# A sliding-window attention and MLP block on one core: the last chunk's output finished by VectorE and plain stores, its PSUM places, the bias matmul, the tile adds of chunk 1, and a new written order

## The chip, the cores and the metric

The kernel runs on one core of a Trainium2 chip. The metric is the device time of one execution in microseconds, as the median of several runs; lower is better. The core's engines each work through their own list of instructions in order: PE (TensorE, matmuls), DVE (VectorE), ACT (ScalarE), POOL (GpSimd) and SP (SyncE, which issues DMAs here). They wait for each other by semaphores.

## What is computed

With x of 2048 rows (positions) by 640, the output is x plus an attention branch plus an MLP branch, both on the layer-normed rows xn. The attention has 32 heads of 20; each position looks at itself and 7 earlier positions, 2 apart.

```python
xn = _layernorm(x, axis=-1)
q, k, v = (xn @ wqkv) split into 32 heads of 20
idx = pos[:, None] - 2 * arange(8)[None, :]
logits = einsum("bhsd,bhswd->bhsw", q, k[idx]) * 20 ** -0.5   (masked where idx < 0)
A = einsum("bhsw,bhswd->bhsd", softmax(logits), v[idx]) @ wo
B = gelu(xn @ w1 + b1) @ w2 + b2
return x + A + B
```

All inputs and the output are bfloat16; w1 is 640 by 1536, w2 is 1536 by 640.

## The kernel before, in words

The 2048 rows are worked in four chunks of 512 (n = 0 to 3), each of four blocks of 128 rows. Features lie on the partitions, rows along the free dimension: xnT, qT, kT, vT and the output of attention oT are each five tiles of 128 features by 512 rows. The feature order of q, k, v is permuted so that four partitions hold one head's features in every tile, 20 in five tiles.

For each chunk:

- Statistics (bn_stats on DVE for chunks 0 and 1, ACT sums for 2 and 3), xn, and its transposition: by PE in chunk 0, by DMA transposes issued on SP (L293) in the others.
- q, k, v projections: five matmuls into a PSUM tile from the pool psA (4 places, L102), cast to SBUF by ACT (`do_pj`, `do_pc`, L340 and L404; chunk 0 in smaller pieces, L353 to L399).
- Products of q and the shifted k on DVE (`do_qk`, L437), 8 shifts in two tiles `half[0]` and `half[1]` of 4 shifts by 5 feature tiles by 512 rows; each instruction does half a chunk's rows for 4 shifts.
- The sum over a head's features: some of the five feature tiles are first added on DVE (`do_pa`, L469: tile 1 onto tile 0 and 3 onto 2 in one instruction; `do_pb`, L474), the rest is summed on PE by matmuls with the 0/1 matrix `head_of` (`do_lg`, L483). `LEVEL` says for each chunk how many adds come first: level 0 leaves five tiles to PE (40 matmuls), level 1 three (24), level 2 two (16), level 3 one (8). Level 1 has four `pa` instructions on DVE, level 2 two `pb` more, level 3 four `pb` more. These matmuls have 32 output rows each; the four blocks go to four different sets of 32 rows.
- Softmax: maximum and subtraction on DVE (L524, L530), exponent on ACT (L540), sums on DVE (L544, L546), reciprocal by Ln and Exp on ACT (L552, L553), product on DVE (L558). The weights `attn` are then spread over the partitions by four DMAs per chunk on SP (`do_xd`, `do_xs`, L577), in chunks 1 and 3 into rows of x_sb that are no longer needed.
- Products with the shifted v on DVE (`do_av`, L592, eight per chunk, into the same two `half` tiles) and their sums (`do_add`, L601, three, and `do_ot`, L606), which give oT.
- The MLP: 12 hidden tiles, five matmuls each (`do_f1`, L613), gelu on ACT (`do_ge`, L629).
- Output of chunks 0 to 2: transposed, T = w2 times hidden plus wo times oT in five pieces (`do_t`, L708), with the bias added by ACT (`do_u`, L711), turned by a DMA transpose on SP (`do_ut`, L715), and added onto the output in memory by an accumulating DMA on POOL (`do_ud`, L720). The output rows have been set to x by a plain DMA earlier (`do_xp`, L302).
- Output of chunk 3: rows on the partitions, per block 17 matmuls of 512 columns ("lo", L656) and 17 of 128 columns ("hi", L661). Blocks 0 and 1 are cast by ACT (`do_oc`, L668, L669) and added onto the output by accumulating DMAs on POOL (`do_od`, L673); their rows have been set to x by `do_xp` of chunk 3 and had b2 added by another accumulating DMA (`do_xb`, L306). Blocks 2 and 3 are added to x + b2 by DVE (`direct`, L680; x + b2 is made in place by `do_xl`, L310) and stored by plain DMAs on SP (L729, L733) and ACT (L744). The "lo" of block 0 and the "hi" of blocks 0 and 1 share the two-bank PSUM tile that the logits use (psL); the "hi" of blocks 2 and 3 share one place of psA, in which the first matmul alone opens the bank (`opened`).

The order of the instructions on PE, DVE, ACT and SP is written out by hand: the string `ORDER` is a list of pieces, and each piece emits its instructions in that order, so that each engine's list is the pieces that use it, in turn. `pj123`, for instance, is projection 2 (v), tile 3 of chunk 1; `lg2` the logit matmuls of chunk 2; `av110` a v product of chunk 1; `ot1` its oT; `f12_5` the hidden tile 5 of chunk 2; `t104` the last piece of T (with oT) for output tile 0 of chunk 1; `o324` the last piece (with oT) of block 2 of chunk 3; `ohi` all "hi" matmuls of block 3. POOL's instructions are placed by the framework. PSUM has eight banks: psA 4, psL 2, psO 2.

Of the kernel before, what the change touches and what calls it, by code (L numbers as in the profile page):

```python
# [11 lines left out]
ALU = mybir.AluOpType  # L12
AX = mybir.AxisListType
BF16 = mybir.dt.bfloat16
# [15 lines left out]
LASTB = S // P - 1  # L30
DIRECT = 2
WARM = 10
RB = 32
# [3 lines left out]
LEVEL = (1, 0, 2, 3)  # L37
# [6 lines left out]
tp01a gb3 tp01b tc01a tc01b gb4 gd gc0 ge tb hj100 st02a st02 rs02 st03a gc1 st03 rs03 xn02 tp02 gc4 ho b1 xn03 st11a  # L44
st13a st10a st12a st10 hc100 st11 hj102 tp03 st13 tc02 tc03 st12 hj101 hc101 hj110 hc110 hc102 hj010 pk rs1 rc1 hj012
hc012 xn12 tc12 hj112 hc112 hj011 hj111 hc010 qk000 xn10 tc10 hc111 hj210 hc210 hc011 hj200 qk001 hc200 xn11 tc11
hj212 hc212 qk010 pad11 hj202 f10_5 hj201 f10_10 xn13 hc202 hc201 f10_4 f10_0 ge0_5 f10_7 ge0_0 tc13 pj102 pa010 ge0_7
pc102 pa001 qk011 pj111 pc111 pj112 pj113 pc112 pa000 pa011 lg0 mask m0a mx0a ge0_4 pc113 ge0_10 ex0a pj103 pc103
pj104 pc104 ldx m0b mx0b ex0b ss0a ri0a pj110 pc110 ss0b ri0b pj114 pc114 pj100 pc100 ld2 pj101 at0a at0b xd0 pc101
qk110 qk100 su22 hj211 hc211 f10_1 pj121 su23 ge0_1 qk101 f10_6 qk111 ge0_6 f10_8 su21 ge0_8 su20 pc121 xs0 f10_9  # L50
f10_2 f11_7 ge0_9 ge0_2 ng2 ge1_7 f10_3 f11_9 pj124 lg1 av030 av000 ldo t040 av001 sq23 sq22 ge0_3 sq21 pc124 sq20 rs2
rc2 av031 av010 m1 f11_2 xp1 av011 av021 av020 mx1 ad00 t000 t041 xn22 tc22 pj123 pc123 xn23 tc23 f11_0 ge1_0 ge1_2
t042 xn21 tc21 f10_11 ge0_11 xn20 tc20 t001 t002 f11_5 ge1_5 pad12 ge1_9 f11_10 ge1_10 t003 ex1 ss1 pj122 f11_11 pj120
pc120 t043 pc122 pj210 pc210 ri1 at1 pj214 pc214 ad01 xp0 xd1 pj220 pc220 pj211 pc211 xp2 su30 ad02 ot0 pj201 pc201
pj204 pc204 su31 xs1 pj212 pc212 pj224 pj213 pc224 pj202 su32 su33 ng3 av111 pc213 pj203 sq32 t044 u04 av110 av121 xp3
av130 av100 t004 u00 ut00 sq31 pj200 pc200 t010 av101 t011 av120 t012 t013 t020 sq30 av131 t014 u01 ut01 sq33 f11_1
rs3 rc3 t021 t022 t023 t024 t030 t031 t032 t033 xn31 t034 tc31 ad10 pad21 xn33 tc33 ad11 pc203 ad12 ot1 ud00 f11_4
ud01 pc202 qk201 ge1_1 ge1_11 xn30 qk211 qk200 f11_8 f12_11 f12_9 qk210 pa211 tc30 pa200 pa210 xn32 tc32 pad22 ge1_8
ge2_9 pa201 f12_3 ge2_11 f11_6 ge1_6 ge1_4 f12_7 pad31 pb212 u02 pj320 pc320 ge2_7 pj304 pc304 pj311 pc311 pb202 pj313
pc313 pj312 pc312 pj222 u03 pc222 xl pj302 pc302 pj301 pj310 pj300 pc310 ge2_3 f13_2 pc300 pc301 pj314 pc314 pj322  # L60
pj303 pc303 pj321 lg2 f11_3 ge3_2 ge1_3 qk310 m2 ut02 f13_8 ge3_8 xb3 f12_5 pa301 t100 pc322 f13_6 t120 pj221 t101
t102 ge2_5 mx2 t121 f12_8 qk300 ex2 ss2 ri2 pa300 t103 pc221 ut03 ut04 ud02 at2 xd2 qk311 xs2 t104 ge2_8 f13_9 ge3_9
t122 t123 u10 f13_10 ge3_10 f13_7 ge3_7 qk301 ud03 pa311 pa310 f13_1 t110 ge3_1 ge3_6 t111 t112 t113 pj323 f12_1 pb302
pj223 pb312 pb304 pc223 pc321 ud04 pb314 t114 u11 pc323 ut10 ut11 f13_0 lg3 ud10 av200 t124 u12 t140 t141 m3 mx3 t130
t131 av210 ut12 t142 ex3 ss3 t143 pj324 av230 ri3 at3 t132 t133 t134 t144 ge3_0 av211 u13 av201 av220 f12_0 ge2_0
ge2_1 pc324 f13_4 ut13 f13_3 f12_4 av221 av231 ad20 ad21 u14 xd3 f13_5 ge2_4 ge3_3 ut14 o310 f12_6 ad22 ot2 ge3_5
ge3_4 o311 o312 ud11 ud12 ud13 ud14 f12_2 xs3 ge2_6 ge2_2 f12_10 pad32 ge2_10 o320 t210 t211 t212 t200 t201 t202
f13_11 ge3_11 t203 t204 t213 t214 u20 ut20 ud20 u21 ut21 ud21 av311 av301 t220 t221 t222 t230 av310 av321 o321 t223
t224 u22 ut22 ud22 t231 t232 t233 t234 u23 ut23 ud23 o330 o331 t240 t241 t242 o300 o301 o313 av330 av320 av300 av331
ad31 t243 t244 u24 ut24 ud24 ad30 o322 o323 ad32 ot3 o302 o303 o314 o304 o324 o332 dc dd o333 o334 ohi oclo ochi oc31  # L70
od31 oc30 ochd od30
# [4 lines left out]
def kernel(  # L76
# [37 lines left out]
    outp = ctx.enter_context(tc.tile_pool(name="outp", bufs=2))  # L114
# [7 lines left out]
    b_rt = consts.tile([RB, P], BF16, name="b_rt")  # L122
# [173 lines left out]
    def rows(n):  # L296
        cs = slice(n * BPC, min((n + 1) * BPC, LASTB + 1 - DIRECT))
        return cs, out_sd.rearrange("(b p) d -> p b d", p=P)[:, cs, :]
# [5 lines left out]
    def do_xb(n):  # L304
        cs, dst = rows(n)
        nc.gpsimd.dma_start(dst, b2bc[:].unsqueeze(1).to_broadcast([P, cs.stop - cs.start, D]), accum_op=ALU.add)  # L306

    def do_xl():
        rows_ = x_sb[:, LASTB + 1 - DIRECT :, :]
        nc.vector.tensor_tensor(  # L310
            out=rows_, in0=rows_, in1=b2bc[:].unsqueeze(1).to_broadcast([P, DIRECT, D]), op=ALU.add
        )
# [149 lines left out]
    def do_b1():  # L462
        nc.vector.tensor_copy(bT[:], tiles["tb"][:, 0 : FT + KT])
# [420 lines left out]
```

## Time and profile before

The median of 3 runs is 209.16 us (208.89 to 209.57). The profile shows one execution in detail.

| what | value |
|---|---|
| time of the profiled execution | 209.39 us |
| its span, first to last instruction | 207.2 us |
| granted TensorE clock | 1.000 |
| ACT_TABLE_LOAD on ACT (L174) | x12, 15.4 us |
| DVE q products (L437) | x16, 44.4 us |
| DVE v products (L592) | x32, 45.6 us |
| DVE sums to oT (L601) | x12, 33.6 us |
| DVE tile adds (L469) | x12, 14.1 us |
| accumulating stores on POOL (L720) | x15, 19.3 us |

The page gives each engine's busy time and its share of the span, then the busy share of 40 slices in tenths, then a chain of waits traced back from the last instruction. Matmuls are pipelined: each is shown with its depth (379 ns for 512 columns), while the next starts earlier, so for the pace one takes the starts of neighbours. In a timeline row the columns are start, length, engine, line, operation, out<-in, shapes and count, and in brackets the idle time before the row with what ended it.

### The profile page before, as it was taken

The numbers are of one execution on the slowest core, as the hardware profiler recorded it, in microseconds if no ns is written. First come the engines' busy times: TensorE is split into PE (matmuls) and PEld (weight loads), VectorE is DVE, ScalarE is ACT, GpSimd is POOL, SyncE is SP. The second block draws the span as 40 slices with busy tenths as digits, with TensorE's granted clock in tenths as the row PEclk, the third lists the DMA queues.
The fourth block names the chain that finished last, engine by engine and source line by source line (L and its number), as shares of the span: only waits on it lengthen the run. The fifth ranks groups of instructions, "written<-read, shape, count | busy, mean of one in ns | idle before, by whom it ended". The sixth has DMA issues, their size and how long they took to land.

```text
span 207.2 us, 2936 instructions
## 1 busy us (share of the span) xinstructions
PE 201.7 (97%) x1137; PEld 106.8 (52%) x1156; DVE 182.6 (88%) x155; ACT 126.4 (61%) x232; POOL 23.9 (12%) x36
## 2 busy tenths in 40 slices
PE   8999999999999999999999999999999999999993
PEld 3999654644444555444455544444444444444552
DVE  2889994799799899999999989999899999999611
ACT  5778967999879877658685537571658621220120
POOL 2000000000000000420002400002040220224050
PEclk9999999999999999999999999999999999999999
DMA  6995879186063358479324800073472970285455
GB/s 211 389 395 180 60 209 394 39 187 209 0 186 67 130 118 211 103 99 86 69 27 52 75 3 0 0 156 73 53 69 45 157 110 3 51 76 51 54 37 115
DMA packets 36607, 23.56 MB, mean 114 GB/s; under 512 B 24946, under 2 KB 34418, under 8 KB 36594
## 3 DMA queue, kind: packets, MB, share of 16 engines
q1 hardware_dynamic: 26464, 18.91, 36.2%
q0 software_dynamic: 8480, 2.62, 16.5%
q10 hardware_dynamic: 1650, 1.84, 2.5%
q8 instruction: 9, 0.15, 0.3%
q14 instruction: 4, 0.03, 0.1%
HBM read 10.00 MB, written 5.24 MB: 74 GB/s over the span
## 4 chain that ended last, share of the span: by engine, by line
PE 68%; DVE 14%; ACT 8%; DMA 6%; issue 1%; SPq 0%; DVEq 0%; ACTq 0%
PE T L708 18%; PE hps L613 15%; PE pps L340 15%; DVE half L592 10%; PE gps L384 6%; PE lo L656 5%; DMA x_sb<-attn 3%; DMA xnT<-xn 3%; PE idle L450 2%; ACT hT L629 2%; PE tail L656 2%; PE L L483 1%; ACT trash L222 1%; PE gps L353 1%; DVE half L601 1%
## 5 line engine op out<-in xcount | busy, mean ns | idle before, releaser
L613 PE MATMUL hps<-xnT,w_sb 128*128 128x512 bf16 x236 | 55.5, 379 | 0.4 <-ACT hT L629 0.2
L437 DVE TENSOR_TENSOR half<-qT,kT 128x5120 bf16<-128x5120 bf16 x16 | 44.4, 2820 | 2.0 <-PE L L483 1.0
L708 PE MATMUL T<-hT,w_sb 128*128 128x512 bf16 x173 | 41.9, 379 | 0.4 <-issue 0.2
L613 PEld LDWEIGHTS <-w_sb 128*128 128x128 bf16 x240 | 23.3, 98 | 27.9 <-issue 0.9
L720 POOL DMA_DIRECT2D out_dram<-x_sb x15 | 19.3, 1286 | 92.2 <-DMA x_sb<-x_sb 91.5
L629 ACT ACTIVATE hT<-hps,bT 128x512 bf16<-128x512 f32 x36 | 23.8, 689 | 9.0 <-PE hps L613 9.0
L708 PEld LDWEIGHTS <-w_sb 128*128 128x128 bf16 x180 | 17.4, 98 | 21.0 <-issue 0.4
L592 DVE TENSOR_TENSOR half<-vT,ax 128x2560 bf16<-128x2560 bf16 x16 | 23.0, 1484 | 2.5 <-ACT vT L404 2.5
L711 ACT ACTIVATE x_sb<-T,bT 128x512 bf16<-128x512 f32 x15 | 10.3, 690 | 20.9 <-PE T L708 20.9
L592 DVE TENSOR_TENSOR half<-vT,x_sb 128x2560 bf16<-128x2560 bf16 x16 | 22.6, 1485 | 0.2 <-DMA x_sb<-attn 0.2
L601 DVE TENSOR_TENSOR half<-half,half 128x5120 bf16<-128x5120 bf16 x8 | 22.3, 2820 | 0.1
L340 PE MATMUL pps<-xnT,wv_sb 128*128 128x512 bf16 x73 | 18.4, 379 | 0.1
L708 PE MATMUL T<-oT,wo 128*128 128x512 bf16 x75 | 18.3, 379 | 0.0
L340 PE MATMUL pps<-xnT,wq_sb 128*128 128x512 bf16 x74 | 17.8, 379 | 0.1
L340 PE MATMUL pps<-xnT,wk_sb 128*128 128x512 bf16 x72 | 17.5, 379 | 0.2
L174 ACT ACT_TABLE_LOAD x12 | 15.4, 1283 | 0.9 <-PEq L868 0.7
L469 DVE TENSOR_TENSOR half<-half 128x2048 bf16<-128x2048 bf16 x12 | 14.1, 1218 | 0.0
L264 ACT ACTIVATE xn<-x_sb,nmr,rstd 128x640 bf16<-128x640 bf16 x12 | 11.0, 921 | 4.1 <-DVE nmr L254 2.8
L340 PEld LDWEIGHTS <-wv_sb 128*128 128x128 bf16 x75 | 8.8, 117 | 7.6
L340 PEld LDWEIGHTS <-wq_sb 128*128 128x128 bf16 x75 | 8.7, 118 | 7.6 <-issue 0.6
L340 PEld LDWEIGHTS <-wk_sb 128*128 128x128 bf16 x75 | 8.8, 117 | 7.4
L404 ACT CAST kT<-pps 128x512 bf16<-128x512 f32 x15 | 8.7, 581 | 6.1 <-PE pps L340 6.1
(104 smaller groups left out, 239.1 us busy)
## 6 DMA issues: line engine op xcount, KB each, us to landing
w_sb<-in_B_w_dram SPq DMA_DIRECT2D x4, 960.0 KB, 10.2
ax<-attn SPq DMA_DIRECT2D x8, 256.0 KB, 4.8
x_sb<-attn SPq DMA_DIRECT2D x8, 256.0 KB, 4.6
out_dram<-x_sb POOLq DMA_DIRECT2D x15, 128.0 KB, 3.8
x_sb<-in_A_x_dram SPq DMA_DIRECT2D x1, 1280.0 KB, 7.6
out_dram<-x_sb ACTq DMA_DIRECT2D x2, 640.0 KB, 5.3
wq_sb<-in_A_wqkv_dram SPq DMA_DIRECT2D x1, 800.0 KB, 4.8
wk_sb<-in_A_wqkv_dram SPq DMA_DIRECT2D x1, 800.0 KB, 6.9
```

Of the source, the lines that this page charges most:

```text
L174: nc.scalar.preload_act_table_set(name)
L340: nc.tensor.matmul(ps[:], lhsT=wqkv_p[which][:, ti, to, :], rhs=xnT[:, ti, :], start=(ti == 0), stop=(ti == KT - 1),)
L384: nc.tensor.matmul(ps[:, to - a, :], lhsT=wqkv_p[which][:, ti, to, :], rhs=tiles["xnT", 0][:, ti, pair * 2 * P : (pair + 1) * 2 * P], star ...
L437: nc.vector.tensor_tensor(out=half[h][:, :, :, cs], in0=q[:, :, at].unsqueeze(1).to_broadcast([P, W // 2, KT, 2 * P]), in1=window(k, h, at ...
L469: nc.vector.tensor_tensor(out=even, in0=even, in1=odd, op=ALU.add)
L592: nc.vector.tensor_tensor(out=half[h][:, :, :, cs], in0=window(qkv_tile(n, 2), h, cs), in1=ax_view(n)[:, j, ws, :].unsqueeze(2).to_broadca ...
L601: nc.vector.tensor_tensor(out=a, in0=a, in1=b, op=ALU.add)
L613: nc.tensor.matmul(ps[:], lhsT=w1_sb[:, ti, ft * P : (ft + 1) * P], rhs=tiles["xnT", n][:, ti, :], start=(ti == 0), stop=(ti == KT - 1),)
L629: nc.scalar.activation(hT, tiles["hps", n, ft][:], ACT.Gelu_apprx_tanh, bias=bT[:, ft : ft + 1], scale=1.0)
L656: nc.tensor.matmul(out_ps(bl, False), lhsT=lhs, rhs=rhs[:, 0:CH], start=pc == 0 and k == 0, stop=final)
L708: nc.tensor.matmul(ps[:], lhsT=lhs, rhs=rhs, start=pc == 0 and k == 0, stop=pc == 4 and k == len(srcs) - 1)
L720: nc.gpsimd.dma_start(dst, src, accum_op=ALU.add)
```

## The change

- `LEVEL` of chunk 1 goes from 0 to 1: four `pa` pieces (L469) are new, `lg1` has 24 matmuls for 40.
- All four blocks of chunk 3 are finished as blocks 2 and 3 were: DVE adds PSUM and x + b2 (`do_dc`) and a plain DMA stores the block (`do_dd`); `do_oc`, `do_od` and their tiles go. `half[1]` has room for four blocks instead of two. `do_xl` now makes x + b2 for the four blocks in two pieces; `do_xb` and the `do_xp` of chunk 3 go.
- Every "lo" and "hi" has a PSUM place of its own: block 0 the two banks of psL, blocks 1 and 2 the four places of psA, block 3 the two of psO.
- The bias rows are turned by a plain matmul with the identity instead of a transpose, from a tile of 128 rows whose unused rows are zero.
- `ORDER` is a new list throughout; it is cut to its last lines here.

```diff
--- before.py
+++ after.py
@@ -27,48 +27,45 @@
 EPS = 1e-5
 MASKED = -1e9
 MW = 16
-LASTB = S // P - 1
-DIRECT = 2
 WARM = 10
-RB = 32
 TURNED = 4
 PARTS = (2, 1, 1, 1)
 
-LEVEL = (1, 0, 2, 3)
+LEVEL = (1, 1, 2, 3)
 ACT_STATS = (2, 3)
 
 COLS = ((0, 2), (2, 4), (4, 5))
 
 ORDER = """
...
-t224 u22 ut22 ud22 t231 t232 t233 t234 u23 ut23 ud23 o330 o331 t240 t241 t242 o300 o301 o313 av330 av320 av300 av331
-ad31 t243 t244 u24 ut24 ud24 ad30 o322 o323 ad32 ot3 o302 o303 o314 o304 o324 o332 dc dd o333 o334 ohi oclo ochi oc31
-od31 oc30 ochd od30
...
+u20 ut20 ud20 t234 u23 t210 t211 t212 t213 t214 t220 t221 t222 t223 t224 u21 ut21 o312 o313 o321 u22 ut22 o330 o322
+ud21 o331 t240 t241 t242 o323 t243 t244 o332 o333 ot3 o303 o304 ud22 o324 dl0 o314 u24 ut23 ut24 ud23 ud24 dl2 o334
+dh0 dd0 dh2 dd2 ohi dl1 dh1 dd1 dl3 dh3 dlo dhi
 """.split()
 
 
@@ -111,7 +108,6 @@
     axp = ctx.enter_context(tc.tile_pool(name="axp", bufs=1))
     otp = ctx.enter_context(tc.tile_pool(name="otp", bufs=1))
     hp = ctx.enter_context(tc.tile_pool(name="hp", bufs=18))
-    outp = ctx.enter_context(tc.tile_pool(name="outp", bufs=2))
 
 
     x_sb = wts.tile([P, NCH * BPC, D], BF16, name="x_sb")
@@ -119,7 +115,7 @@
     w1_sb = wts.tile([P, KT, F], BF16, name="w1_sb")
     w2_sb = wts.tile([P, FT, D], BF16, name="w2_sb")
     wo2 = wts.tile([P, KT, D], BF16, name="wo2")
-    b_rt = consts.tile([RB, P], BF16, name="b_rt")
+    b_rt = consts.tile([P, P], BF16, name="b_rt")
     nc.gpsimd.memset(b_rt[:], 0.0)
     b2bc = consts.tile([P, D], BF16, name="b2bc")
     wqkv_v = A_wqkv.rearrange("(t p) n -> p t n", p=P)
@@ -294,21 +290,17 @@
 
 
     def rows(n):
-        cs = slice(n * BPC, min((n + 1) * BPC, LASTB + 1 - DIRECT))
+        cs = slice(n * BPC, (n + 1) * BPC)
         return cs, out_sd.rearrange("(b p) d -> p b d", p=P)[:, cs, :]
 
     def do_xp(n):
         cs, dst = rows(n)
         (nc.scalar if n else nc.sync).dma_start(dst, x_sb[:, cs, :])
 
-    def do_xb(n):
-        cs, dst = rows(n)
-        nc.gpsimd.dma_start(dst, b2bc[:].unsqueeze(1).to_broadcast([P, cs.stop - cs.start, D]), accum_op=ALU.add)
-
-    def do_xl():
-        rows_ = x_sb[:, LASTB + 1 - DIRECT :, :]
+    def do_xl(pair):
+        rows_ = x_sb[:, (NCH - 1) * BPC + 2 * pair : (NCH - 1) * BPC + 2 * pair + 2, :]
         nc.vector.tensor_tensor(
-            out=rows_, in0=rows_, in1=b2bc[:].unsqueeze(1).to_broadcast([P, DIRECT, D]), op=ALU.add
+            out=rows_, in0=rows_, in1=b2bc[:].unsqueeze(1).to_broadcast([P, 2, D]), op=ALU.add
         )
 
 
@@ -456,11 +448,11 @@
             )
 
     def do_tb():
-        tiles["tb"] = psL.tile([P, 2 * W * P], BF16, tag="L", name="tb")
-        nc.tensor.transpose(tiles["tb"][:, 0:RB], b_rt[:], ident[0:RB, 0:RB])
+        tiles["tb"] = psL.tile([P, W, P], F32, tag="L", name="tb")
+        nc.tensor.matmul(tiles["tb"][:, 0, 0 : FT + KT], lhsT=b_rt[:], rhs=ident[:, 0 : FT + KT], start=True, stop=True)
 
     def do_b1():
-        nc.vector.tensor_copy(bT[:], tiles["tb"][:, 0 : FT + KT])
+        nc.vector.tensor_copy(bT[:], tiles["tb"][:, 0, 0 : FT + KT])
 
     def do_pa(n, h, c):
 
@@ -633,16 +625,12 @@
 
 
     def out_ps(bl, hi):
-        first = lambda: psL.tile([P, W, P], F32, tag="L", name="tail")
-        if bl == 0 or (hi and bl == 1):
-            ps = get("tail", first)[:].rearrange("p w c -> p (w c)")
-            return ps[:, CH + bl * P : CH + (bl + 1) * P] if hi else ps[:, 0:CH]
-        key = "hi" if hi else ("lo", bl)
-        pool, tag = (psO, "o") if key == ("lo", BPC - 1) else (psA, "acc")
-        ps = get(key, lambda: pool.tile([P, CH], F32, tag=tag, name="hi" if hi else "lo"))
-        return ps[:, (bl - BPC + DIRECT) * P : (bl - BPC + DIRECT + 1) * P] if hi else ps[:]
-
-    opened = set()
+        if bl == 0:
+            both = get("first", lambda: psL.tile([P, W, P], F32, tag="L", name="both"))[:].rearrange("p w c -> p (w c)")
+            return both[:, CH:D] if hi else both[:, 0:CH]
+        pool, tag = (psO, "o") if bl == BPC - 1 else (psA, "acc")
+        ps = get(("out", bl, hi), lambda: pool.tile([P, CH], F32, tag=tag, name="hi" if hi else "lo"))
+        return ps[:, 0 : D - CH] if hi else ps[:]
 
     def do_o(bl, pc, parts):
         n, cs = NCH - 1, slice(bl * P, (bl + 1) * P)
@@ -651,34 +639,25 @@
         else:
             srcs = [(tiles["oT", n][:, t, cs], wo2[:, t, :]) for t in range(KT)]
         for k, (lhs, rhs) in enumerate(srcs):
-            final = pc == 4 and k == len(srcs) - 1
-            if "lo" in parts:
-                nc.tensor.matmul(out_ps(bl, False), lhsT=lhs, rhs=rhs[:, 0:CH], start=pc == 0 and k == 0, stop=final)
-            if "hi" in parts:
-                bank = bl // 2
-                first = bank not in opened
-                opened.add(bank)
+            for hi in parts:
                 nc.tensor.matmul(
-                    out_ps(bl, True), lhsT=lhs, rhs=rhs[:, CH:D], start=first, stop=final, skip_group_check=True
+                    out_ps(bl, hi),
+                    lhsT=lhs,
+                    rhs=rhs[:, CH:D] if hi else rhs[:, 0:CH],
+                    start=pc == 0 and k == 0,
+                    stop=pc == 4 and k == len(srcs) - 1,
                 )
 
-    def do_oc(bl):
-        osb = outp.tile([P, D], BF16, tag="osb", name="osb")
-        tiles["osb", bl] = osb
-        nc.scalar.copy(osb[:, 0:CH], out_ps(bl, False))
-        nc.scalar.copy(osb[:, CH:D], out_ps(bl, True))
-
-    def do_od(bl):
+    def do_dc(bl, hi):
+
+        b, cs = (NCH - 1) * BPC + bl, slice(CH, D) if hi else slice(0, CH)
+        room = half[1][:].rearrange("p w t c -> p (w t c)")[:, bl * D : (bl + 1) * D]
+        nc.vector.tensor_tensor(out=room[:, cs], in0=out_ps(bl, hi), in1=x_sb[:, b, cs], op=ALU.add)
+
+    def do_dd(bl, cs, eng):
         b = (NCH - 1) * BPC + bl
-        nc.gpsimd.dma_start(out_sd[b * P : (b + 1) * P, :], tiles["osb", bl][:], accum_op=ALU.add)
-
-    def direct(bl, hi):
-
-        b = (NCH - 1) * BPC + bl
-        room = half[1][:].rearrange("p w t c -> p (w t c)")[:, (bl % 2) * D : (bl % 2 + 1) * D]
-        cs = slice(CH, D) if hi else slice(0, CH)
-        nc.vector.tensor_tensor(out=room[:, cs], in0=out_ps(bl, hi), in1=x_sb[:, b, cs], op=ALU.add)
-        return room, out_sd[b * P : (b + 1) * P, :]
+        room = half[1][:].rearrange("p w t c -> p (w t c)")[:, bl * D : (bl + 1) * D]
+        eng.dma_start(out_sd[b * P : (b + 1) * P, cs], room[:, cs])
 
 
 
@@ -720,28 +699,9 @@
         nc.gpsimd.dma_start(dst, src, accum_op=ALU.add)
 
 
-    def do_dc():
-        direct(BPC - 2, False)
-        tiles["dc"] = direct(BPC - 2, True)
-
-    def do_dd():
-        room, dst = tiles["dc"]
-        nc.sync.dma_start(dst, room)
-
-    def do_oclo():
-        room, dst = direct(BPC - 1, False)
-        nc.sync.dma_start(dst[:, 0:CH], room[:, 0:CH])
-
     def do_ohi():
         for pc in range(5):
-            do_o(BPC - 1, pc, ("hi",))
-
-    def do_ochi():
-        tiles["hi"] = direct(BPC - 1, True)
-
-    def do_ochd():
-        room, dst = tiles["hi"]
-        nc.scalar.dma_start(dst[:, CH:D], room[:, CH:D])
+            do_o(BPC - 1, pc, (True,))
 
     pieces = {}
 
@@ -749,7 +709,7 @@
         assert name not in pieces
         pieces[name] = lambda: fn(*args)
 
-    for name in "tb b1 mean1 ho ldx ld2 ldo xl dc dd oclo ohi ochi ochd mask pk".split():
+    for name in "tb b1 mean1 ho ldx ld2 ldo ohi mask pk".split():
         piece(name, locals()[f"do_{name}"])
     for u, a, b, eng in (("a", 0, 2, "ve"), ("b", 2, KT, "se")):
         for bl in range(2):
@@ -804,7 +764,8 @@
                     piece(f"pc{n}{which}{to}", do_pc, n, which, to)
         for which in (1, 2):
             piece(f"pad{n}{which}", do_pad, n, which)
-        piece(f"xp{n}", do_xp, n)
+        if n < NCH - 1:
+            piece(f"xp{n}", do_xp, n)
         for h in range(2):
             for pair in range(2):
                 piece(f"qk{n}{pair}{h}", do_qk, n, pair, h)
@@ -835,13 +796,18 @@
                 piece(f"ut{n}{s}", do_ut, n, s)
                 piece(f"ud{n}{s}", do_ud, n, s)
             continue
-        piece(f"xb{n}", do_xb, n)
+        last = BPC - 1
+        for pair in range(2):
+            piece(f"xl{pair}", do_xl, pair)
         for bl in range(BPC):
             for pc in range(5):
-                piece(f"o{n}{bl}{pc}", do_o, bl, pc, ("lo",) if bl == BPC - 1 else ("lo", "hi"))
-            if bl < BPC - DIRECT:
-                piece(f"oc{n}{bl}", do_oc, bl)
-                piece(f"od{n}{bl}", do_od, bl)
+                piece(f"o{n}{bl}{pc}", do_o, bl, pc, (False,) if bl == last else (False, True))
+            piece(f"dl{bl}", do_dc, bl, False)
+            piece(f"dh{bl}", do_dc, bl, True)
+            if bl < last:
+                piece(f"dd{bl}", do_dd, bl, slice(0, D), nc.sync)
+        piece("dlo", do_dd, last, slice(0, CH), nc.sync)
+        piece("dhi", do_dd, last, slice(CH, D), nc.scalar)
 
     engines = {getattr(mybir.EngineType, e) for e in ("PE", "DVE", "Activation", "SP")}
     with tc.manual_schedule(engines=engines):
```

## Prediction

> **What bounds the kernel now.** I read the page's busy times and slices first, then the chain of waits, then the timeline of TensorE around the four groups of logit matmuls (L483), then the timeline of VectorE.
>
> ```profile
> span 207.2 us, 2936 instructions
> ...
> PE 201.7 (97%) x1137; PEld 106.8 (52%) x1156; DVE 182.6 (88%) x155; ACT 126.4 (61%) x232; POOL 23.9 (12%) x36
> ...
> PE   8999999999999999999999999999999999999993
> ...
> DVE  2889994799799899999999989999899999999611
> ...
> PE 68%; DVE 14%; ACT 8%; DMA 6%; issue 1%; SPq 0%; DVEq 0%; ACTq 0%
> ```
>
> PE is at 9 in every slice but the first and last: the end of the kernel is PE's last matmul (203.80 us) plus a tail of 3.4 us. DVE is at 9 nearly as often, so it is a second bound with little room. Where the two meet is in the timelines:
>
> ```profile
> 32.47 1.48 PE L483 MATMUL L<-half,head_of 128*32 128x512 bf16 x24
> ...
> 52.36 2.34 PE L483 MATMUL L<-half,head_of 128*32 128x512 bf16 x40
> ...
> 120.93 1.05 PE L483 MATMUL L<-half,head_of 128*32 128x512 bf16 x16
> ...
> 147.05 0.62 PE L483 MATMUL L<-half,head_of 128*32 128x512 bf16 x8
> ...
> 196.24 0.38 PE L656 MATMUL lo<-wo,oT 128*128 128x512 bf16 x1
> ```
>
> ```profile
> 24.02 2.35 DVE L469 TENSOR_TENSOR half<-half 128x2048 bf16<-128x2048 bf16 x2
> ...
> 34.00 0.29 DVE L494 TENSOR_TENSOR L<-L,mask 32x128 f32<-32x128 f32 x1 [2.62 <-PE L L483]
> ...
> 41.20 11.03 DVE L437 TENSOR_TENSOR half<-qT,kT 128x5120 bf16<-128x5120 bf16 x4 [0.97 <-ACT qT L404]
> ...
> 193.58 1.49 DVE L606 TENSOR_TENSOR oT<-half 128x2560 bf16<-128x2560 bf16 x1
> ...
> 203.84 0.29 DVE L680 TENSOR_TENSOR half<-hi,x_sb 128x128 bf16<-128x128 f32 x1 [0.26 <-PE hi L661]
> ```
>
> The reader is to see two things. The logit matmuls are cheap each: 24 of them take 1.41 us until the next matmul starts (33.88), a spacing of 59 ns. And DVE delivers the last chunk's oT at 195.07, 1.1 us before PE first uses it at 196.24: that is all the slack at the end.
>
> **The change on PE.** Chunk 1's logits take 3 instead of 5 tiles per half: 16 matmuls fewer, 16 x 0.059 = 0.94 us. The rows bound it: 40 against 24 matmuls is 2.34 - 1.48 = 0.86 by their busy times, 2.50 - 1.41 = 1.09 by the start of the next matmul (54.86 and 33.88). I take **0.95 us removed**. The bias step is one small matmul before and after (0.11). The blocks of the last chunk keep their matmul counts. Nothing else goes or comes on PE, but the whole order is rewritten.
>
> I laid PE's order of both kernels out as a running sum, with spacings from the chain of waits: 512 columns 0.216 (20 in 4.32), 256 columns 0.109 (90 in 9.82), 128 columns 0.055. The sum starts at the first transpose (5.45 us) and comes to 196.64 before and 195.68 after. Before, position 26.29 (first L483) ran at 32.47, 46.08 at 52.36, 114.26 at 120.93, 140.25 at 147.05: PE lags its own sum by 6.2, 6.3, 6.7, 6.8 us, 5.45 being the start. So PE lost 1.5 us in 200, and its next gain is only in work. With the same lags the new order puts the logits of chunks 0 to 3 (sums 25.21, 49.53, 115.25, 141.87) at **31.4, 55.8, 121.9 and 148.7**, the first use of the last oT (189.62) at **196.55**, and PE's end at 203.80 - 0.95 = **202.85**.
>
> **The change on DVE.** Added ahead of the last oT: four tile adds (L469), spaced 1.14 (2.35 less 1.22 for two), 4.56 us; a second bias-to-rows add (L310, 0.82 long, about 0.75 to the next). That is **5.3 us more**. It must be found in DVE's idle time, because PE's need for that oT moves only from 196.24 to 196.55. After the oT, two blocks more are added from PSUM (2 x (0.69 + 0.28), L680); PE still has 6 us to run there, so they lie beside it.
>
> So I walked DVE's new order by hand against those PE times, with spacings from the rows: L437 2.74, L592 1.40, L469 and L474 1.14, three L601 plus L606 9.94, maximum and subtraction 1.14 each, softmax sums 1.4, attn 1.14.
>
> Chunk 0: starts its products at 15.8 as before, done 31.3; logits at 31.4 (32.47 before), mask at 32.9 (34.0 before), softmax 6.2 us as before, 39.1. Chunk 1's products wait for the last q, k cast: PE's sum 33.12 instead of 34.20, so 40.1. Four products and four adds: 55.6, where PE comes at 55.8. After, half 0 is free when 12 logit matmuls (0.7) are through: 56.75, against 53.73 before. From there eight products with softmax between, three adds: oT of chunk 0 at 82.9, its first use 76.42 + 6.5 = 82.9. Chunk 1: oT at 106.7 with one of chunk 2's products put in front. Chunk 2: its last add 121.7, PE 121.9; the second half of the bias add; the maximum 123.15; chunk 3's products and adds done at 148.1, PE 148.7. Chunk 2's oT 175.2 (first use 175.9). Chunk 3's oT: 175.2 + 11.2 + 9.9 = **196.45**, needed at 196.55.
>
> DVE's idle in this walk, 31.3 to 196.45: 1.6 at the mask, 0.9 at chunk 1's products, 1.1 behind its logits, 0.7 and 0.4 behind the later ones, 4.7 in all, where the trace has some 8.6 in the same stretch (2.6, 1.0, 1.5, 0.7 ahead of attn, 1.0, 1.0 and drains). So the new order pays the 5.3 us by starting chunks 0 and 1 a microsecond earlier and idling 4 us less, and arrives with 0.1 to 0.2 us to spare at five places. A walk of 100 spacings has no such accuracy: small misses become PE stalls. They can't make it earlier than the work allows; I take **0.2 us** in all, with ends 0 and 1.7 (below).
>
> **ACT, queues, stores.** ACT loses four casts (0.59, 0.27, 0.59, 0.28) and one DMA issue: beside PE, worth nothing; if ACT is late anywhere it is at chunk 1's exponent, behind two gelus whose matmuls end at 65.2 and a table load (1.28): 68.8, when DVE wants it at 68.9. Table loads stay at 12. POOL loses three accumulating stores (L306 1.35, L673 1.78 for two), all off the path. SP gains two plain stores behind the last transpose (1.19 to issue, done some 4 us ahead of them); nothing is queued behind them but the last block's store. On SP chunk 1's attn loads (L577) and the x stores that free their rows come in the same turn as before, with 2 us to spare.
>
> The Trainium skill ("SBUF — State Buffer", Who interferes with whom) says that a VectorE instruction with two SBUF inputs contends with a GpSimd instruction that reads SBUF; by that, dropping L306 beside the L592 products would give DVE up to 1.35 us, an estimate from that row's length. The trace does not bear it out: L592 takes 1484 ns with ax and 1485 with x_sb as input, the latter while L306 and L720 ran, and L720 takes 1282 to 1305 whatever DVE does. The sum takes nothing for it.
>
> **Tail.** Before: last matmul 203.80, add to 204.13, store issued on ACT 204.16, landed 1.8 later, 205.96, end 207.2. After, the same three steps. The last adds of blocks 1 and 3 stand in line: 0.69 + 0.28 + 0.69 between the end of block 1's matmuls (2.0 us ahead of PE's end) and block 3's last, done by then. So 3.4 us again, bounded by -0.3 (two accumulating stores of 4.2 us no longer in flight) and +1.1 (block 1's store is issued 1.0 us ahead of PE's end and takes the 4.2 of L729; but that one ran beside them, and the 128 KB L733 took 2.2).
>
> **Sum.** The profiled execution took 209.39 for its span of 207.2; the median is 209.16. 209.16 - 0.95 + 0.2 = **208.4 us**, range of this case 208.1 to 208.8. A measurement here tells some 0.3% (0.63 us) from no change, so the forecast lies just past that bound.
>
> **Rivals.**
> 1. **DVE becomes the bound** (slower). The waits for ACT that this trace shows and my walk leaves out come again: 0.7 ahead of attn (L558) and 1.0 ahead of a first product for a vT cast (L592). For: five meetings without slack, and an exponent with 0.1. Against: my walk has these casts done early. Price 1.7: 209.16 - 0.95 + 1.7 = 209.9. It is a loss from 0.95 us on. If none of the idle time were saved, the oT would come at 200.4 and the time be 213.
> 2. **The stores crowd the end** (no change). Two blocks' stores move from POOL's queue to SP's, three of 160 KB within 2 us; the last ones come 0.5 to 1.1 late: 208.7 to 209.3, say 208.9. The Trainium skill ("DMA: Bandwidth & Descriptors", Issuing engines are not separate DMA queues) has all queues on the same 16 engines, so that the queue would not matter. Against: the trace's DMA slices show 64 to 323 GB/s while the end's stores run, and at the 230 of their middle the 480 KB take 2.1 us, which is done before the last store lands.
> 3. **Better than its work**: the new order also loses less than PE's 1.5 us, and the tail shortens by 0.3: 207.8.
>
> **Chances.** Forecast 0.47 (of it 0.33 below 208.53, 0.14 above); rival 1 0.25 (of it 0.19 over 209.79); rival 2 0.16; rival 3 0.12. Faster by over 0.3%: 0.33 + 0.12 = 0.45. Slower: 0.19. Same: 0.14 + 0.16 + 0.06 = 0.36. The range, 207.8 to 210.0, leaves out half of rival 3 and the upper half of rival 1, some 0.18.
>
> **What would show it.** L483 has 72 matmuls and PE's busy time falls by about 1 us; L469 is x16, DVE's busy time about 190. Right: the first L483 near 31.4, 55.8, 121.9, 148.7, PE idle nowhere over 0.2, the last oT at 196.4. Rival 1: DVE idle 0.5 or more ahead of L558, L592 or L544, and PE waiting for DVE at L483 or at the first wo matmul of a chunk. Rival 2: more than 3.4 us from PE's last matmul to the end. I would be wrong altogether if PE waited for ACT or for the transposes in the rewritten order: outside the stretch from 40 to 69 us the sum takes PE's PSUM places and the transposed inputs to be ready, as they were before.

## The result and the profile after

The changed kernel takes 211.66 us in the median of four runs (210.06 to 212.07); the kernel before, measured beside it, 209.02 us (208.88 to 209.57). The ratio is 1.0112, with a 95% interval of 1.0090 to 1.0134: slower by about 1.1%, where 208.4 us was forecast. In a later measurement (experiment 8) the ratio came out at 0.9989 [0.9963, 1.0014]: the loss is not of one size, and why is part of what follows. Some executions of most kernels here, of the kernel before too, have a mean granted clock of 0.99 and take 2 to 3 us more; three of the four executions of this measurement are such, and the fourth, at 1.00, took 210.06 us, which is still above the slowest one before.

The profiled execution took 211.6 us, its span is 209.6 us (207.2 before). The page of the changed kernel, its busy times, two of its slice rows and the engines of its chain:

```profile
span 209.6 us, 2919 instructions
...
PE 203.6 (97%) x1140; PEld 106.3 (51%) x1140; DVE 189.4 (90%) x164; ACT 125.4 (60%) x228; POOL 20.9 (10%) x33
...
PE   8999999999999599999999999999999999999994
...
PEclk9999999999999799999999999999999999999999
...
PE 93%; DMA 3%; ACT 3%; issue 0%; DVE 0%
```

DVE's busy time is where the prediction put it (about 190). PE's should have fallen by 1 us and rose by 1.9; but these two sums compare badly, for the trace of before has 1137 matmul records beside 1156 weight loads, this one 1140 beside 1140. Plainer is one slice: the fourteenth (68 to 73 us) has PE at 5 and the granted clock at 7. Before, PE was at 9 in that slice. In the chain DMA has 3% (6% before), and all of it is now one transfer, xnT<-xn.

The timeline of PE in the changed kernel around that slice (start, length, engine, line, operation, shape, count; in brackets the idle time ahead and what ended it):

```profile
66.05 2.75 PE L687 MATMUL T<-hT,w_sb 128*128 128x512 bf16 x12
70.95 2.30 PE L332 MATMUL pps<-xnT,wv_sb 128*128 128x512 bf16 x5 [2.15 <-DMA xnT<-xn]
73.05 1.83 PE L332 MATMUL pps<-xnT,wq_sb 128*128 128x512 bf16 x5
74.72 1.46 PE L332 MATMUL pps<-xnT,wk_sb 128*128 128x512 bf16 x6
```

PE is ready for the first projection of chunk 2 at 68.8 and waits 2.15 us for the transposed rows xnT. Then the next five matmuls take 2.10 us and the five behind them 1.67, where five of 512 columns take 1.08 at full clock: 3.77 instead of 2.16, that is 1.6 us lost to the clock. Together 3.75 us. The windows of the same trace, one microsecond each, show the clock in the column behind POOL's busy time (with DMA share and GB/s behind it):

```profile
69.00:70.00 1.00, 0.00 (x0) 0.00 (x0) 0.93 (x3) 0.40 (x2) 0.00 (x0) 1.00 1.06 394
70.00:71.00 1.00, 0.05 (x1) 0.08 (x2) 1.00 (x2) 0.62 (x2) 0.00 (x0) 0.91 0.21 69
71.00:72.00 1.00, 1.00 (x3) 0.37 (x4) 1.00 (x2) 0.00 (x0) 0.00 (x0) 0.50 0.00 0
```

While PE idles the DMA engines carry 394 GB/s; right behind that the clock is at half.

What fills the DMA engines is on ACT's queue. ACT's timeline in the changed kernel (ACTq is a DMA issue on ACT's queue), and the chain of waits of the same stretch:

```profile
65.17 0.69 ACT L621 ACTIVATE hT<-hps,bT 128x512 bf16<-128x512 f32 x1
65.18 0.99 ACTq L298 DMA_DIRECT2D out_dram<-x_sb  x2
...
67.75 1.02 ACT L532 ACTIVATE e<-L 128x1024 bf16<-128x1024 f32 x1
```

```profile
64.28 0.82 ACT xn L260
65.10 0.02 issue
65.11 5.70 DMA xnT<-xn
70.81 0.14 issue
70.95 4.15 PE pps L332 x11
```

The two stores of x rows for chunks 1 and 2 (`xp1`, `xp2`, 640 KB each) stand in the new order behind chunk 1's exponent, which runs at 67.75. They are issued at 65.18. That is 0.07 us after the last DMA transposition of chunk 2, which then lands 5.70 us after its issue; the three of this chunk ahead of it took 2.4 to 2.5. Before, the same two stores were issued apart, at 56.09 and 74.06, with all four transpositions of the chunk between them:

```profile
56.09 0.42 ACTq L302 DMA_DIRECT2D out_dram<-x_sb  x1
...
74.06 0.43 ACTq L302 DMA_DIRECT2D out_dram<-x_sb  x1
```

```profile
59.08 7.27 SPq L293 DMA_TRANSPOSE xnT<-xn  x4
```

### The profile page after: what moved, and what is told of

It reads as the page before. It is cut to its first block, busy times and chain, and to the rows that moved or that the text cites. A ratio compares the mean times of both kernels' runs of the same rounds, so it can differ in the third digit from the quotient of the medians.

```text
span 209.6 us, 2919 instructions
## 1 busy us (share of the span) xinstructions
PE 203.6 (97%) x1140; PEld 106.3 (51%) x1140; DVE 189.4 (90%) x164; ACT 125.4 (60%) x228; POOL 20.9 (10%) x33
## 4 chain that ended last, share of the span: by engine, by line
PE 93%; DMA 3%; ACT 3%; issue 0%; DVE 0%
PE T L687 25%; PE pps L332 24%; PE hps L605 22%; PE gps L376 7%; PE lo L643 5%; DMA xnT<-xn 3%; PE idle L442 2%; PE both L643 2%; PE L L475 2%; PE gps L345 1%; PE hi L643 1%; ACT hT L621 1%; ACT xn L260 1%; PE tp L277 1%; ACT L170 1%
## 5 line engine op out<-in xcount | busy, mean ns | idle before, releaser
L687 PE MATMUL T<-hT,w_sb 128*128 128x512 bf16 x180 | 43.1, 379 | 0.0
L584 DVE TENSOR_TENSOR half<-vT,ax 128x2560 bf16<-128x2560 bf16 x16 | 23.2, 1483 | 0.5 <-ACT hT L621 0.4
L584 DVE TENSOR_TENSOR half<-vT,x_sb 128x2560 bf16<-128x2560 bf16 x16 | 22.6, 1482 | 0.0
L332 PE MATMUL pps<-xnT,wv_sb 128*128 128x512 bf16 x75 | 19.5, 395 | 2.1 <-DMA xnT<-xn 2.1
L461 DVE TENSOR_TENSOR half<-half 128x2048 bf16<-128x2048 bf16 x16 | 18.7, 1217 | 0.0
L332 PE MATMUL pps<-xnT,wq_sb 128*128 128x512 bf16 x75 | 18.6, 388 | 0.0
L332 PE MATMUL pps<-xnT,wk_sb 128*128 128x512 bf16 x75 | 18.0, 380 | 0.0
L396 ACT CAST qT<-pps 128x512 bf16<-128x512 f32 x15 | 8.7, 586 | 13.4 <-PE pps L332 13.4
L687 PEld LDWEIGHTS <-wo 128*128 128x128 bf16 x75 | 7.3, 98 | 8.8
```

Source lines behind the costliest of these rows:

```text
L332: nc.tensor.matmul(ps[:], lhsT=wqkv_p[which][:, ti, to, :], rhs=xnT[:, ti, :], start=(ti == 0), stop=(ti == KT - 1),)
L461: nc.vector.tensor_tensor(out=even, in0=even, in1=odd, op=ALU.add)
L584: nc.vector.tensor_tensor(out=half[h][:, :, :, cs], in0=window(qkv_tile(n, 2), h, cs), in1=ax_view(n)[:, j, ws, :].unsqueeze(2).to_broadca ...
L687: nc.tensor.matmul(ps[:], lhsT=lhs, rhs=rhs, start=pc == 0 and k == 0, stop=pc == 4 and k == len(srcs) - 1)
```

## The experiments

**Theory**: the loss is the collision of the two stores with that transposition, and the clock that falls behind PE's wait. **Rivals**: the rewritten order has PE ask for these rows too early, whatever the stores do; DVE has become the bound; the first measurement was a matter of its executions. In all but experiments 4 and 6 only places in the order (and in 10 the issuing engine) change; all ratios are to the kernel before on the same chip.

### 1 and 2: the stores later, the stores earlier

```diff
 # e1_stores_behind_ri1
-... pj121 ex1 xp1 xp2 pc121 ss1 av010 pad12 ri1 at1
+... pj121 ex1 pc121 ss1 av010 pad12 ri1 xp1 xp2 at1
 # e2_stores_early
-... pc120 sq22 f10_3 ...  pj121 ex1 xp1 xp2
+... pc120 sq22 xp1 xp2 f10_3 ...  pj121 ex1
```

> Edit to the changed kernel: in the written order the two 640 KB stores of x (chunks 1 and 2, issued on ACT) stand behind chunk 1's reciprocal instead of behind its exponent, so that they are issued at about 70.3 us instead of 65.18. Theory A (the two stores take the DMA engines while the last transposition of chunk 2 is under way, and its late landing stalls PE): the transposition issued at 65.1 lands at about 67.5 (2.4 us, as the other three) instead of 70.8, PE waits nowhere over 0.2 us, the third group of logit matmuls starts at 121.9 (125.5 in the changed kernel), the granted clock stays at 1.0 throughout, time 207.7 to 208.3, which is faster than the kernel before. Rival B (the fourth transposition is late for a reason of its own, its place in SP's queue or its late input): the wait of 2.1 us stays, time 211.6. Rival C (the collision is real but other stalls of the new order stand behind it): wait gone, time 208.7 to 209.5.

> Edit to the changed kernel: the same two stores are moved the other way, to about 50 us, behind the first of the square sums of chunk 2, where the trace shows the DMA engines nearly idle. Theory A: the same as with the later place, transposition landed at 67.5, no PE wait, 207.7 to 208.3. Rival B: 211.6. If the later place were slower than this one by 0.3 us or more, the stores there would be in the way of the next chunk's attn loads.

Measured: 208.68 us, ratio 0.9971 [0.9938, 1.0004], and 208.35 us, ratio 0.9974 [0.9942, 1.0006]. In experiment 1 the stores are issued at 70.82, PE starts the projection at 68.80 without a wait for a DMA, and the clock is 1.00 all the way. In experiment 2 PE does not wait for xnT either; its profiled execution lost 1.5 us at its start, where PE waits for the load of wq. Taking the stores away in either direction takes the wait away, so PE does not ask too early. Neither ratio is clear of 1, though, and experiment 1 missed its 207.7 to 208.3: its profile has a new wait of PE, 0.28 us for a cast of q on ACT at 72.5.

### 3: the collision put into the kernel before

```diff
 # e3_before_stores_at_transpose (from the kernel before)
-... m1 f11_2 xp1 av011 ...  ge1_5 pad12 ...  pc211 xp2 su30
+... m1 f11_2 av011 ...  ge1_5 xp1 xp2 pad12 ...  pc211 su30
```

> Edit to the kernel before: its two x stores of chunks 1 and 2 (56.1 and 74.1 us) are put side by side behind the gelu that follows the last xn of chunk 2, so that they are issued at about 65 us, as in the changed kernel. Theory A: the last transposition of chunk 2 lands near 70.5 instead of 67.5, PE, which wants it at 69.5, waits about 1 us, and what the clock loses comes on top (0 to 1.5): 210 to 211.7. Rival B: no wait appears, 209.1.

Measured: 211.14 us, ratio 1.0077 [1.0036, 1.0118]. The stores are issued at 63.90 and 64.42, the last transposition at 64.91, and it lands 5.90 us later. PE's timeline in this kernel:

```profile
70.95 2.33 PE L340 MATMUL pps<-xnT,wk_sb 128*128 128x512 bf16 x10 [1.48 <-DMA xnT<-xn]
```

Ten matmuls in 2.33 us: the clock did not fall behind these 1.48 us. So the stores do the same to the kernel before, without any other part of the change.

### 4: PE kept busy through the wait

Ten matmuls of 512 columns on constants, whose result nobody reads, are put ahead of that projection (`fill`).

```diff
 # e4_filled_wait
+    def do_fill():
+        ps = psA.tile([P, CH], F32, tag="acc", name="fill")
+        for _ in range(10):
+            nc.tensor.matmul(ps[:], lhsT=ones[:, 0:P], rhs=ones[:], start=True, stop=True)
-... t043 av101 pj223 pj201
+... t043 av101 fill pj223 pj201
```

> Edit to the changed kernel: ten matmuls of 512 columns on constants, whose result nobody reads, stand ahead of the projection that waits for the transposition; they take 10 x 0.216 = 2.2 us, the length of the wait. Theory A1 (the granted clock falls to 0.7 in that slice because PE stood still): the clock stays at 1.0, the matmuls behind the wait are spaced 0.216, and the time is that of the changed kernel less 1.4 to 1.6: 210.1. Rival A2 (the clock falls for another reason, or costs nothing): 211.6 to 212.

Measured: 210.69 us, ratio 1.0073 [1.0041, 1.0105]; span 208.5. PE's timeline and a window of this kernel:

```profile
69.22 2.35 PE L453 MATMUL fill<-const-bfloat16-1.0 128*128 128x512 bf16 x10
71.40 1.24 PE L332 MATMUL pps<-xnT,wv_sb 128*128 128x512 bf16 x5
```

```profile
70.00:80.00 10.00, 10.00 (x48) 5.21 (x46) 9.90 (x8) 6.01 (x14) 0.00 (x0) 1.00 0.58 144
```

The clock stays at 1.00 here and the five projections behind the fill take 1.08, as the theory has it. But this does not settle what the fall of the clock costs, and 210.1 was expected. The collision was smaller in this execution: the transposition's last packets ran at 69.6 us, so that its rows were in at about 70.1 (an estimate; in the changed kernel the landing came 0.5 us behind the last packet, 70.31 and 70.81), while the fill held PE until 71.4. Without the fill PE would have waited about 1.0 us, from 69.22 on. And the changed kernel without a fill, on the same chip (experiment 8), takes 209.76 us, with a clock of 1.00 in most runs. So the fill is no remedy here, and what it prevents is not shown by its time. The size of the fall is read elsewhere: 3.77 us instead of 2.16 in the changed kernel's trace, and in its first measurement 210.06 us at a clock of 1.00 against 211.60 to 212.07 at 0.99.

### 5: one store instead of two

```diff
 # e5_one_store_early
-... pc120 sq22 f10_3 ...  pj121 ex1 xp1 xp2
+... pc120 sq22 xp2 f10_3 ...  pj121 ex1 xp1
```

> Edit to the changed kernel: only the store of chunk 2's x goes to about 50 us; that of chunk 1's x stays behind the exponent and is issued at about 65.2. Theory A (the stores' traffic delays the transposition): with half the bytes, 640 KB or some 1.65 us at the 390 GB/s of the trace, the last transposition lands at 69.2 at the latest instead of 70.8, PE waits 0.1 to 0.5 us, time 0.1 to 0.6 us above the kernel with both stores early. Rival (any store there delays it as much): wait 2.1 us as before.

Measured: 209.28 us, ratio 0.9998 [0.9969, 1.0026]. The chain and PE's timeline in this kernel:

```profile
66.15 4.02 DMA xnT<-xn
```

```profile
70.30 1.25 PE L332 MATMUL pps<-xnT,wv_sb 128*128 128x512 bf16 x5 [0.46 <-DMA xnT<-xn]
```

The same transposition lands 2.4 (experiment 7), 4.0 and 5.7 us after its issue with no, one and two stores beside it: 1.65 us for each. 640 KB at the 390 GB/s of these windows take 1.68. So in landing it comes as late as if each store went ahead of it whole. The packets of the changed kernel's trace show it otherwise. SP's queue is q1, ACT's q10; packets, MB and share of the 16 engines from 66.95 to 68.7 us, from 68.7 to 69.45 and from 69.45 to 71:

```profile
q10 hardware_dynamic: 350, 0.43, 71.2%
q1 hardware_dynamic: 640, 0.16, 41.0%
...
q10 hardware_dynamic: 230, 0.29, 105.7%
...
q10 hardware_dynamic: 242, 0.29, 50.7%
q1 hardware_dynamic: 32, 0.00, 1.2%
```

All 640 data packets of the transposition (256 bytes each) run in the first stretch and end at 68.67. That is 3.56 us after the issue, where an undisturbed one needs 1.92 (experiment 7). Its 32 closing packets, of 4 bytes, follow an undisturbed transposition's data within 0.1 us; here they wait until 69.49 to 70.31, when the stores end too, and the landing comes 0.5 us behind them. In experiment 5 the data end after 3.55 us as well, and the closing packets after 3.56. So the first store delays the data by 1.6 us, and the second only the closing packets, by another 1.6. PE was ready at 68.80: nearly all of its wait was for a transfer whose data packets had already run.

Experiment 5's time, 1.1 us above that of experiment 7, is more than the 0.1 to 0.6 expected; its profile has only the 0.46 us of wait here, and 1.3 us for the load of wq at the start.

### 6 and 7: what the removed matmuls are worth; the early stores again

Experiment 6 is experiment 2 with chunk 1's tile adds left to PE, as before the change; 7 is experiment 2 once more.

```diff
 # e6_level0_stores_early
-LEVEL = (1, 1, 2, 3)
+LEVEL = (1, 0, 2, 3)
-... hj212 pa111 pa110 pa101 su21 ...  f10_3 pa100 ge0_3
+... hj212 su21 ...  f10_3 ge0_3
```

> Edit to the kernel with both stores early: chunk 1's logits again from five tiles (40 matmuls), its four tile adds on VectorE left out, the order else the same. If PE is the bound of the new order (the prediction's sum), this costs what the prediction took for the 16 matmuls, 0.95 us: about 0.9 us above the kernel with both stores early, equal to the kernel before less its tail. If VectorE is the bound, it is faster, by up to the 4.6 us of the adds.

> The kernel with both x stores early once more, on the chip of the other runs of this call, for a tighter interval against the kernel before and beside the changed kernel. Theory A: 0.4 to 0.6% faster than before (PE's sum is 0.95 us shorter and the tail about 0.3), PE's median wait at the projection zero. If it is within 0.3% of the kernel before, the order loses elsewhere what the logit matmuls save.

Measured: 209.37 us, ratio 1.0003 [0.9973, 1.0033], with level 0; 208.14 us, ratio 0.9948 [0.9918, 0.9977], with the changed kernel's level 1. Chunk 1's logits start in PE's timelines:

```profile
55.86 2.34 PE L475 MATMUL L<-half,head_of 128*32 128x512 bf16 x40
58.13 0.82 PE L687 MATMUL T<-hT,w_sb 128*128 128x512 bf16 x3
```

```profile
56.17 1.48 PE L475 MATMUL L<-half,head_of 128*32 128x512 bf16 x24
57.58 0.82 PE L687 MATMUL T<-hT,w_sb 128*128 128x512 bf16 x3
```

The first block is experiment 6, the second 7: the next matmul starts 2.27 and 1.41 us behind the first logit matmul, 0.86 apart. The medians are 1.2 apart. With DVE 4.6 us less busy (184.9 against 189.5) experiment 6 is the slower one, so DVE is not the bound.

### 8 and 9: the changed kernel again

The kernel is the changed one as it stands.

> The changed kernel itself once more, beside the kernel with both stores early on the same chip. Theory A: 3 to 3.7 us above that kernel where the clock falls behind the wait, 1.6 to 2.2 where it does not; the wait of about 2 us ahead of the first projection of chunk 2 is there again.

> The changed kernel as it is, one more look. Theory (two collisions of size that varies): the fourth transposition of chunk 2 lands between 4 and 6 us after its issue, PE waits 1 to 2.2 us for it, and where the granted clock in the ten microseconds behind the wait stays above 0.97 the span is 1 to 2.3 us longer than that of the order with early stores (206.2). Rival (the loss seen in the first profile belongs to that one execution): no wait for xnT, and a span of 206 to 206.5.

Measured: experiment 8, on the chip and beside the same runs of the kernel before as 7: 209.76 us, ratio 0.9989 [0.9963, 1.0014], single runs from 208.59 to 213.38. Its profiled execution (213.38) shows the collision in the same size, a landing after 5.70 and a wait of 2.14, but there the clock stays at 1.00 behind it and falls to 0.89 between 10 and 20 us instead, behind a wait of 2.06 for wq. Experiment 9: 211.61 us, wait 2.13, clock 0.83 from 70 to 80 us. So all three profiled executions have the wait, and two of three the fall of the clock at this place.

The clock's own records in the traces fit this. Every change lies a whole number of 3.41 us behind the first rise: in the changed kernel it rises at 5.97 us, falls at 70.83, 19 times 3.41 later, and is back after 3.41. In the stretch of 3.41 us ahead of a fall PE had idled 2.03 us here, 2.13 in experiment 9, and 2.07 (for wq) in experiment 8. The wait for xnT in experiment 8 lies across a border of two stretches, at 73.67, with 1.42 us ahead of it and 0.72 behind. No fall followed that, nor 1.48 us in experiment 3 or 1.52 in experiment 2. So the same wait of 2.1 us costs the clock or not by where it lies. This is read from the traces at hand; no experiment shifted a wait across a border to see.

But several runs of experiment 8 that were not profiled lie only 1 to 1.3 us above the fastest of 7 (207.63), which is less than the wait; there the collision must be smaller, as it was in the profile of experiment 4, and the expectation of 1.6 us at least does not hold for them. So the rival that the first measurement was a matter of its executions is right as to the size of the loss and wrong as to its cause.

### 10 and 11: the queue or the moment

```diff
 # e10_stores_behind_on_sp: on SP, behind the last transposition
-        (nc.scalar if n else nc.sync).dma_start(dst, x_sb[:, cs, :])
+        nc.sync.dma_start(dst, x_sb[:, cs, :])
-... xn20 tc20 av031 ...  pj121 ex1 xp1 xp2
+... xn20 tc20 xp1 xp2 av031 ...  pj121 ex1
 # e11_stores_behind_cast: on ACT, one place later
-... pj121 ex1 xp1 xp2 pc121 ss1
+... pj121 ex1 pc121 xp1 xp2 ss1
```

> The changed kernel with the two x stores moved from ACT to SP, right behind the last transposition of chunk 2 in SP's own list. They are issued at about 66.3 and 66.9 instead of 65.2, no earlier and much too late to be done before PE needs the transposed rows at 68.8. If what delays the transposition is that the stores come to the DMA engines beside it, on another queue and at the same moment, then here its descriptors stand ahead of theirs: it lands 2.4 to 3.2 us after its issue, PE waits at most 0.1, and the time is that of the early stores, 208.1 to 208.6. Rival (any 1.28 MB in flight between 65 and 69 us slows it, whatever the queue): it lands after 4 us or more, PE waits 0.5 or more, and the time is 209 or more.

> The changed kernel with the two x stores one place later in ACT's list, behind the next cast of a vT tile (L396), still on ACT's queue. That cast waits for matmuls that end at about 66.2, so the stores are issued at about 66.2 to 66.3, as in the order that had them on SP, but on the other queue than the transposition. If the queue decides (descriptors of another queue go ahead of or between those of the transposition), the fourth transposition still lands 4 us or more after its issue and PE waits 0.5 or more: 209 us or more. If the moment decides (1.1 us later is behind the transposition's own data on the DMA engines), it lands 2.4 to 3 after its issue, PE waits at most 0.1, and the time is 207.6 to 208.7. If the stores are issued only where the cast runs (68.7), it is the second case too, and the issue's start tells which.

Measured: 208.61 us, ratio 0.9957 [0.9905, 1.0008] (profiled 207.57), and 208.20 us, ratio 0.9942 [0.9912, 0.9972]. The issues of experiment 11 and what PE does behind them:

```profile
66.80 0.41 ACTq L298 DMA_DIRECT2D out_dram<-x_sb  x1
...
67.25 0.53 ACTq L298 DMA_DIRECT2D out_dram<-x_sb  x1
```

```profile
66.59 2.75 PE L687 MATMUL T<-hT,w_sb 128*128 128x512 bf16 x11
69.18 1.24 PE L332 MATMUL pps<-xnT,wv_sb 128*128 128x512 bf16 x5
```

The last transposition is issued at 65.65 here; the stores come 1.15 us later on the other queue. By the packets of the trace its data move from 66.8 to 67.6 us and the stores' from 67.8 on, and PE does not wait. In experiment 10 they come 1.25 us after it on its own queue, with the same end. In the changed kernel the stores' packets begin at 66.16 us and the transposition's only at 66.99, 1.87 us after its issue instead of 1.2. The bytes, their rate (394 GB/s from 68 to 71 us) and in 11 the queue are those of the changed kernel: what differs, as far as these traces show, is which transfer's packets go first. The profile of experiment 4 lies between: with the same 0.07 us between the issues, the transposition's packets began first there, at 66.86 against 67.29, and were done 1.3 us earlier than in the changed kernel, counted from its issue. The kernel before has such a store itself: `xp0` goes out on SP 1.25 us behind the last transposition (66.40 and 65.15), and PE does not wait. With one name of the order moved past its neighbours the kernel of experiment 11 is faster than both, 0.6% below the one before.

## Why the prediction was wrong, step by step

**What bounds the kernel**: right. PE's chain sets the end, and PE had no slack where the rows came late.

**The change on PE**: right. 0.95 us (0.86 to 1.09) was taken off; the logits of experiments 6 and 7 are 0.86 apart. The places can be read from experiment 10, which has neither the collision nor a wait at the start: the logits start at 31.21, 55.64, 121.56 and 148.35 (forecast 31.4, 55.8, 121.9, 148.7), the last oT is first used at 196.3 (196.55), and PE ends at 202.6 (202.85). In the changed kernel they are at 31.32, 55.75, 125.53 and 152.32: right up to the collision, 3.6 late behind it.

**The change on DVE**: right. The walk's four oT at 82.9, 106.7, 175.2 and 196.45 end in experiment 10 at 82.56, 106.38, 174.99 and 196.26. (The walk's last sum, 175.2 + 11.2 + 9.9, is 196.3 and not the 196.45 written there.) In the changed kernel the last one is done at 200.2, and PE uses it at once; DVE waits longer than in experiment 10 behind the late rows (1.5 us against 0.5 for logits at L516, 2.9 against 0.8 for ACT's statistics at L250). DVE did not become the bound (rival 1). POOL's issue of L306 is gone, and the products beside it take 1483 and 1482 ns where they took 1484 and 1485: taking nothing for it was right.

**ACT, queues, stores**: this step failed. It says that the stores "come in the same turn as before, with 2 us to spare", and so looked at who waits for the stores and priced them at nothing. It did not place them in time, and it did not ask which transfer is in flight when they start. Both ACT stores had been moved past other work, to one place, and two things were needed to see where they land: that ACT's DMA issues go out when nothing ahead of them on ACT waits any more (65.18 is 0.04 us behind the end of the last matmuls that a gelu ahead waits for, 65.14; in experiment 11, 66.80 is 0.05 behind the end of those that the cast ahead waits for, 66.75), here 2.57 us before the exponent that stands ahead of them in the list runs (67.75); and that the fourth transposition of chunk 2 is issued just then (65.11), with 3.7 us until PE needs it. The lines for it were in the trace of before: ACT's issues at 56.09 and 74.06 beside SP's transposes from 59.08 on. The price would have been two stores of 640 KB at about 390 GB/s, 3.3 us more than the 2.4 of an undisturbed transposition: landed at 70.8 for a need at 68.8, a wait of 2, where 2.15 was measured. The prediction named this among its conditions ("the transposed inputs to be ready, as they were before", "I would be wrong altogether if PE waited for ACT or for the transposes") but gave it no chance, and the stretch from 40 to 69 us, which it excepted, was walked for q, k casts and DVE alone.

The second half of the loss, the clock, was nowhere in the prediction: PE's waits were counted at their own length. The Trainium skill ("TensorE: Matmul & The Clock Gate", What's actually happening) has the clock at half after an idle window of about 3.4 us. The 0.50 at 71 to 72 us agrees with the half; the idle time was 2.15 us here, so it can fall behind less than that figure (experiments 8 and 9 show when it did).

**Tail**: the direction of rival 2 was wrong. From PE's last matmul to the end take 3.1 us, not 3.4 (206.55 to 209.6; in experiment 10 202.6 to 205.7), the lower bound of the step. The three plain stores at the end cost nothing that shows.

**Sum**: 209.16 - 0.95 + 0.2 forecast 208.4. The order without the collision takes 208.14 (experiment 7) and 208.20 (experiment 11). They lie 0.2 to 0.3 us below the forecast, about what the tail gained. The changed kernel has 2.15 + 1.6 us more in its profile. The collision as the cause of the wait is shown from three sides: taken away (1, 2, 7, 10, 11), put in elsewhere (3), halved (5). That the wait in turn drops the clock fits all the traces and was not tested apart. Left open is why unprofiled executions of the changed kernel lose 1 to 1.6 us in experiment 8 and some 3.5 in the first measurement. A store whose packets begin some tenths of a microsecond later, as in experiment 4's profile, and a fall of the clock that comes or does not, would do for both; no run shows the packets without a profile.

## What to carry to other kernels

Place every moved DMA issue in time, by when the last wait ahead of it on its engine ends and not by where it stands in the list, and look which transfer that the bound engine waits for is issued within a microsecond of it; where the first store's packets began ahead of the transposition's, each 640 KB store delayed the landing by its whole 1.65 us. A bulk store without a deadline goes ahead of such a transfer by many microseconds or behind it by one. Where PE waits 2 us, allow for some 1.6 more from the clock: it came in two of the three profiles of the changed kernel.

## What the runs showed of the hardware

- A DMA issue on ACT's queue ran 2.57 us ahead of the activation that precedes it in the list, and in experiment 11 2.4 us ahead of the cast that precedes it (66.80 and 69.21).
- A transposition of 160 KB took 2.4 us to land alone, 4.0 beside one 640 KB store issued about when it was, 5.7 beside two, 5.9 where both were issued up to 1.0 us ahead of it; where they were issued 1.15 us behind it on another queue, or 1.25 on its own, PE did not wait for it. The Trainium skill ("DMA: Bandwidth & Descriptors", Queues, rings and completion order) has each DMA engine go round the queues that have work, a packet from each in turn; the trace counts 673 packets on SP's queue from 65.1 to 71 us, nearly all of them the transposition's, and 1056 on ACT's, the stores', so packet by packet the transposition would be through after some two thirds of the stores, an estimate from these counts. For its data the trace is near this: they ended at 68.67 us, when 574 of the 1056 had begun. Its 32 closing packets of 4 bytes came only with the stores' end, 70.31 against 70.34, which turns alone do not explain, and it is these that the landing followed, by 0.5 us.
- The granted clock fell to half, for 3.41 us, where PE had idled 2.03 to 2.13 us within one stretch of 3.41 us counted from the clock's first rise (changed kernel, experiments 8 and 9), and not where it had idled 1.42 to 1.52 us in one (experiments 2, 3 and 8).
- The load of wq at the start came 0.9 to 2.1 us late in some profiled executions (experiments 2, 5, 8 and 11) and 0 to 0.7 us late in the others: enough to hide an effect of half a per cent in a single run.
